# A delta-rule attention block followed by a SiLU MLP: in the first chunk, two of the four batches are joined first and alone, and two pieces of w_in meet their 128 tokens between the joins of the other two

## The chip, the cores and the metric

The kernel runs on one core of a Trainium2 chip. The metric is device time in microseconds; the time before is the median of three runs.

The engines are TensorE (PE; its weight loads are the rows PEld), VectorE (DVE), ScalarE (ACT), GpSimd (POOL) and SyncE (SP), which issues most of the DMAs. Each engine runs its own list of instructions in order, and they meet at semaphores.

## What is computed

```python
# q, k, v: (4, 8, 768, 48) float32; beta: (4, 8, 768)
k_n = k / (norm(k, axis=-1) + 1e-06)
state = zeros(4, 8, 48, 48); y = zeros_like(q)
for t in range(768):
    y[:, :, t] = einsum('bhd,bhde->bhe', q[:, :, t], state)
    v_old = einsum('bhde,bhd->bhe', state, k_n[:, :, t])
    state += beta[:, :, t] * einsum('bhd,bhe->bhde', k_n[:, :, t], v[:, :, t] - v_old)
x = y.transpose(0, 2, 1, 3).reshape(3072, 384)
h = x @ w_in                    # 384 x 2048
g = h * (1 / (1 + exp(-h)))
out = g @ w_out                 # 2048 x 384
```

## The kernel before

**Tiling.** The 768 steps are cut into six chunks of 128 (c), each chunk into two halves of 64 steps (hf). Batches 0 and 1 make group g = 0, batches 2 and 3 group g = 1; a group has 16 heads, and one half of it holds 2 x 64 = 128 tokens. One half of a chunk gives the MLP 256 tokens: 128 of each group. Within a chunk the recurrence becomes a triangular system per head, so the kernel needs the inverse of a triangular matrix for each head.

**Chunk 0, from the inverse to the first outputs.** `invert_first` (L663) inverts the small diagonal blocks on VectorE and turns them with two transposes (L690, L694). Then come the joins, which put the blocks together into the inverse of each half. Each stage is a row of small matmuls on TensorE, 16 or 32 for a group, then copies out of PSUM on ScalarE (L544) and VectorE (L547), one side of the 128 partitions each:

- `corner` (matmuls L717, copies by VectorE L724);
- `turned` (L733) and `straight` (L746), copies into xe_y and into xi;
- `merge_half`, twice (L806): the first merge reads turned's xe_y and writes xe_y, the second reads xe_y and xi and writes xi.

`joins(hf, between)` runs these stages for both groups in turn, corner(0), corner(1), turned(0), turned(1) and so on, and between them does what the list `between` holds (narrowing steps, sizing v on GpSimd by `size_half`). Then `masks` (L1364) cuts the scores of queries with a triangle (four VectorE instructions), `solve(0)` does `inner` (L840, the inverse times v), and `first_outputs` (L884), which makes the 128 tokens of one group in two PSUM banks; a ScalarE copy and a VectorE add (L893) put them into xT. `inner` writes to a zeroed strip (`slab`) and to z.

**The MLP.** `hidden(c, hf)` (L1046) goes through w_in in eight pieces f of 256 columns. A piece is six matmuls of 128 x 128 weights by 256 tokens, two halves of three with a `yield` between; in fp32 each matmul is two passes in the profile, so a half piece is six rows. A silu on ScalarE (L1056) takes the bank to gT. Hidden's banks, and those of the transposes (`turn`, L500), come from two PSUM banks in rotation (M); joins use three (A) and three (CC). `project` (L1090) multiplies by w_out.

**Narrowing.** w_in and w_out arrive as 64-bit numbers and are cut to fp32 piece by piece (`narrow`): two ScalarE instructions (L233, L234), two VectorE ones (L238, L242) and one on GpSimd (L246). `begin_next` starts ScalarE's part of the next piece in the queue, and `fill(n)` does n more of its steps; hidden's piece f needs ("in", f) narrowed. Raw pieces land in the space of tiles that are used later, and a full queue of pieces waits for that space.

**Order.** Nothing is reordered by a scheduler: `pin` (L78) puts each instruction behind the one that the program wrote before it on the same engine, and `in_line` does the same for SP's DMAs. The order is that of the program, and after the joins of half 0 it is a text that `script` (L1509) reads word by word: s is a step of `solve`, jN N matmuls of `joins(1)`, r half a piece of hidden (`run`), fN narrowing steps, b `begin_next`, q the transposes of one batch of chunk 1's queries (their ScalarE copy writes stage, L510), h the sizing of v for half 1. `project` and the steps of later chunks follow in the same text.

**Loads by count.** `pin` counts TensorE's instructions (2 for a transpose, 4 for a matmul); when the count passes the first number in `loads`, that load is issued behind the TensorE instruction reached. The numbers are WINDOW + PACKET * k + an offset, with PACKET 256 and WINDOW 445. The block loads of chunk 0 (`block_in`, L582) and those of k, v and the first two pieces of w_in are issued ahead of that.

## Time and profile before

| | |
|---|---|
| median of three runs | 641.6 us (639.44 to 643.4) |
| span of the profiled execution | 636.1 us, from the first to the last instruction |
| TensorE busy (PE / PEld) | 622.4 us / 547.3 us |
| VectorE / ScalarE / GpSimd busy | 397.5 / 214.3 / 89.9 us |
| mean granted TensorE clock | 0.986 |
| DMA | 54.70 MB, mean 86 GB/s |

The profiled execution has a span of 636.1 us and no time of its own beside it in the table; the median of the runs lies 5.5 us above the span, for what is ahead of the first instruction and behind the last.

How to read the lines that follow. `L840` is a line of the kernel before. A row of the timeline has the start in us from the span's start, the duration, engine, line, operation, the tiles written and read, and in brackets how long the engine was idle just before and who released it. "x6" is a count; rows with a count are merged. The chain of waits is followed back from the last instruction and shows what set the time at each moment; "issue" in it is time in which the engine waited for nothing that the profile shows. PEclk is the clock that TensorE was granted, as a share of full speed.

### The profile page before, as it was taken

Reading aid. Unit: us, or ns where it says so; the run is one execution under the profiler, and the core shown is the slowest. Engines: PE = TensorE matmul, PEld = TensorE weight load, DVE = VectorE, ACT = ScalarE, POOL = GpSimd, SP = SyncE. Lnnn points to the kernel's source line nnn. Section 1 sums busy time; section 2 is a strip of 40 time slices with the busy share of each in tenths; the row PEclk is TensorE's granted clock in tenths of the full one; section 3 lists DMA queues with packets and bytes.
Section 4 is the critical chain, followed back from the end, with each engine's and each line's share of the span. In section 5 each row is a group of like instructions: output and inputs, shape, how many; then the busy total and the mean of one; then the engine's idle time right before and its main releaser. Section 6 shows DMA issues by size and latency. Waiting matters only on the chain.

```text
span 636.1 us, 21387 instructions
## 1 busy us (share of the span) xinstructions
PE 622.4 (98%) x9406; PEld 547.3 (86%) x9406; DVE 397.5 (62%) x910; ACT 214.3 (34%) x500; POOL 89.9 (14%) x92
## 2 busy tenths in 40 slices
PE   7979999999999999999999999999999999999997
PEld 5568788656799989989989989989989989989997
DVE  5786879999677974546974555975455964112112
ACT  3456673423351122451122451122451122441120
POOL 5033721345020020020020010020002000000000
PEclk9779999999999999999999999999999999999999
DMA  7966726350458460459151359232253133010101
GB/s 114 227 159 177 218 67 148 100 99 4 95 105 174 72 104 8 94 107 183 37 91 21 75 124 164 56 84 29 64 117 76 26 75 37 16 38 1 26 0 26
DMA packets 145676, 54.70 MB, mean 86 GB/s; under 512 B 117152, under 2 KB 138912, under 8 KB 145584
## 3 DMA queue, kind: packets, MB, share of 16 engines
q1 hardware_dynamic: 143136, 52.93, 40.5%
q8 instruction: 74, 1.21, 0.8%
q10 hardware_dynamic: 2448, 0.41, 0.4%
q14 instruction: 18, 0.15, 0.1%
HBM read 40.14 MB, written 11.01 MB: 80 GB/s over the span
## 4 chain that ended last, share of the span: by engine, by line
PE 94%; DVE 2%; DMA 1%; issue 1%; ACTq 0%; ACT 0%; POOL 0%; SPq 0%; DVEq 0%; POOLq 0%
PE phid L1046 40%; PE px L1163 17%; PE py L1163 13%; PE po L1090 5%; PE pb_c L840 3%; PE pa L529 2%; PE pb_c L828 2%; PE pyc L919 2%; PE pb_c L1090 2%; PE pb_c L860 2%; PE pyc L906 1%; PE px L782 1%; PE py L782 1%; PE pt L500 1%; DMA sums_of_w<-blocks 1%
## 5 line engine op out<-in xcount | busy, mean ns | idle before, releaser
L1046 PE MATMUL phid<-xT,w_in 128*128 128x256 f32 x1152 | 257.0, 381 | 0.2 <-DVE xT L893 0.2
L1046 PEld LDWEIGHTS phid<-xT,w_in 128*128 128x128 f32 x1152 | 216.4, 190 | 30.2 <-issue 0.9
L1056 ACT ACTIVATE gT<-phid 128x512 f32<-128x512 f32 x88 | 52.5, 597 | 144.8 <-PE phid L1046 140.5
L1144 DVE TENSOR_TENSOR sums_of_g<-gT 128x384 f32<-128x384 f32 (+1 forms) x60 | 30.4, 529 | 65.7 <-ACT gT L1056 55.4
L627 DVE SCALAR_TENSOR_TENSOR rank<-g,step,x 128x31 f32<-128x31 f32 (+15 forms) x124 | 49.8, 401 | 21.7 <-DMA g<-blocks 18.1
L1163 PE MATMUL px<-sums_of_w,sums_of_g 128*128 128x192 f32 x320 | 56.6, 329 | 0.0
L1163 PE MATMUL py<-w_out,sums_of_g 128*128 128x192 f32 x320 | 56.2, 328 | 0.0
L1163 PEld LDWEIGHTS py<-w_out,sums_of_g 128*128 128x128 f32 x320 | 52.3, 190 | 0.3
L1163 PEld LDWEIGHTS px<-sums_of_w,sums_of_g 128*128 128x128 f32 x320 | 52.2, 190 | 0.4
L632 DVE TENSOR_TENSOR x<-x,rank 128x31 f32<-128x31 f32 (+15 forms) x124 | 42.5, 342 | 4.3
L467 POOL TENSOR_TENSOR vf<-vf,n_slot 128x768 f32<-128x768 f32 x10 | 14.8, 1494 | 174.4 <-DMA vf<-in_v_dram 150.4
L544 ACT COPY xT<-pyc 48x128 f32<-48x128 f32 (+2 forms) x126 | 32.7, 260 | 1.7
L488 DVE STREAM_TRANSPOSE kq<-stage 128x512 f32<-128x512 f32 x28 | 28.4, 1115 | 5.2 <-DMA stage<-in_q_dram 5.2
L1163 PE MATMUL py<-w_out,gT 128*128 128x192 f32 x160 | 28.9, 330 | 0.0
L1174 DVE TENSOR_TENSOR o<-o,kept 128x192 f32<-128x192 f32 (+1 forms) x29 | 11.5, 422 | 26.7 <-ACT kept L1171 26.7
L1163 PE MATMUL px<-w_out,gT 128*128 128x192 f32 x160 | 27.9, 327 | 0.0
L1163 PE MATMUL px<-sums_of_w,gT 128*128 128x192 f32 x160 | 27.8, 327 | 0.0
L1163 PEld LDWEIGHTS px<-w_out,gT 128*128 128x128 f32 x160 | 26.5, 190 | 0.6
L550 POOL COPY g<-x 64x256 f32<-64x256 f32 x4 | 5.0, 1242 | 151.9 <-DVE x L635 151.9
L1163 PEld LDWEIGHTS py<-w_out,gT 128*128 128x128 f32 x160 | 26.1, 190 | 0.4
L865 DVE TENSOR_TENSOR state<-state,pb_c 128x384 f32<-128x384 f32 x22 | 11.2, 550 | 24.1 <-PE pb_c L860 24.1
L1163 PEld LDWEIGHTS px<-sums_of_w,gT 128*128 128x128 f32 x160 | 26.2, 190 | 0.1
(222 smaller groups left out, 931.2 us busy)
## 6 DMA issues: line engine op xcount, KB each, us to landing
vf<-in_v_dram SPq DMA_DIRECT2D x48, 96.0 KB, 2.8
out_dram<-o SPq DMA_DIRECT2D x42, 96.0 KB, 2.2
w_out<-in_moe_w_in_dram SPq DMA_DIRECT2D x4, 768.0 KB, 4.7
sums_of_w<-in_moe_w_out_dram SPq DMA_DIRECT2D x4, 768.0 KB, 4.1
blocks<-ap SPq DMA_DIRECT2D x44, 64.0 KB, 1.9
g<-blocks SPq DMA_DIRECT2D x5, 512.0 KB, 3.5
kb<-in_k_dram SPq DMA_DIRECT2D x12, 192.0 KB, 4.2
kb<-in_k_dram SPq DMA_DIRECT2D x24, 96.0 KB, 4.3
```

The lines of the kernel that those rows point to most:

```text
L467: pin(nc.gpsimd.tensor_tensor(out=vf, in0=vf, in1=of, op=ALU.mult))
L488: pin(nc.vector.transpose(out=kqs[c, b][:, :, j, :].rearrange("p a (i m) -> p a m i", i=T), in_=src.rearrange("p a (m d) -> p a m d", d=D) ...
L529: pin(nc.tensor.matmul(pa[e][half, p * n * W : (p + 1) * n * W], lhsT=kq[rows, p, 0, half], rhs=kq[rows, p, js[0] : js[-1] + 1, half], sta ...
L544: return pin(nc.scalar.copy(to, of))
L627: pin(nc.vector.scalar_tensor_tensor(out=tv, in0=g[:, 0:m, m : m + 1].to_broadcast([P, m, n]), scalar=step[:, m : m + 1], in1=x[:, m : m + ...
L632: yield pin(nc.vector.tensor_tensor(out=x[:, 0:m, m:T], in0=x[:, 0:m, m:T], in1=tv, op=ALU.add))
L840: yield pin(nc.tensor.matmul(pz[rows, n * D : (n + 1) * D], lhsT=xis[g][rows, u * H + 2 * p + e, :], rhs=vfs[c][rows, hf, g * HB + u, p, : ...
L1046: pin(nc.tensor.matmul(ph[:, j * GT : (j + 1) * GT], lhsT=w_in[:, a, (2 * f + j) * P : (2 * f + j + 1) * P], rhs=xTs[c, hf][:, a, :], star ...
L1056: pin(nc.scalar.activation(out=hidden_of(c, hf, f), in_=ph[:], func=ACTF.Silu, scale=-0.5 if in_blocks(c) else 0.5))
L1090: pin(nc.tensor.matmul(pos[i][:, 0:DM], lhsT=hidden_of(0, hf, f // 2)[:, at : at + C], rhs=w_outs[f // HFF][:, f % HFF, :], start=(f == 0) ...
L1144: pin(nc.vector.tensor_tensor(out=sums_of_g[:, k, fs], in0=of[0], in1=of[1], op=op))
L1163: pin(nc.tensor.matmul(to, lhsT=at, rhs=quarter(f, *b) if isinstance(b, tuple) else sums_of_w[b][:, f], start=start and f == 0, stop=f == ...
```

## The change

- **Order of chunk 0.** `joins` no longer holds half 0 (nor the corners of half 1). Group 0 goes alone through corner, turned, straight, first merge, second merge, `inner` and `first_outputs`; then group 1 through the same stages. Between group 1's stages stand other things: the corners of half 1 (`corner(0, 1)`, `corner(1, 1)`) and two calls of `early`.
- **`early(f, g)`** multiplies piece f of w_in (f = 0, 1) with the 128 tokens of one group alone: six matmuls by 128 tokens instead of six by 256. `early(0, 0)` stands between corner and turned of group 1, `early(1, 0)` between its first and second merge; `early(0, 1)` and `early(1, 1)` come after its `first_outputs`, each with the silu. `hidden(0, 0)` then begins at f = 2. Each piece has one PSUM bank of M, held from the first call to the second.
- **Masks.** Group 0's two masks go to VectorE right after v's load is issued, ahead of the blocks' inverse; group 1's two go to GpSimd, after group 0's outputs.
- **Sizing of v** (half 0) goes ahead of the memset of `slab` on GpSimd; before it was behind.
- **Loads.** w_in 2 to 5 at packets 2 to 5, then chunk 1's queries at 6 and 7, w_in 6 at 8, w_in 7 at 10, w_out 2 at 11. Before: w_in 2 and 3 at packets 2 and 3, the queries at 4 and 5, w_in 4 to 7 at 6 to 9, w_out 2 at 10.
- **Script.** The head of the text is new: all four query transposes (q) come after the joins of half 1 have begun, where two of them stood ahead; one `r` fewer stands near the beginning of the rest, since four half pieces were done by `early`.

```diff
     def solve(c):
         if c == 0:
-            together(inner(0, 0, 0, CC))
-            together(inner(0, 1, 0, M))
-            yield
-            first_outputs(0)
-            yield
-            first_outputs(1)
-            yield
             together(update(0, 0, 0), update(0, 1, 0))
...
+    def early(f, g):
+        if g == 0:
+            early_banks[f] = bank(M, "phid")
+        ph = early_banks[f]
+        for j in range(2):
+            for a in range(NKT):
+                pin(nc.tensor.matmul(
+                    ph[:, j * GT + g * C : j * GT + (g + 1) * C],
+                    lhsT=w_in[:, a, (2 * f + j) * P : (2 * f + j + 1) * P],
+                    rhs=xTs[0, 0][:, a, g * C : (g + 1) * C], start=(a == 0), stop=(a == NKT - 1),
+                ))
+        if g == 1:
+            silu(0, 0, f, ph)
...
     def hidden(c, hf):
-        for f in range(NFF // 2):
+        for f in range(EARLY if (c, hf) == (0, 0) else 0, NFF // 2):
...
     def masks(g, u):
         to = aps[0, g][1][:, u]
-        pin(nc.vector.tensor_tensor(
+        pin((nc.gpsimd if g == 1 else nc.vector).tensor_tensor(
             out=to, in0=to, in1=above[:].unsqueeze(1).to_broadcast([P, H, W]), op=ALU.mult
         ))
...
     load_v(0)
+    masks(0, 0)
+    masks(0, 1)
...
         (WINDOW + PACKET * 2 + 15, fetch_w_in, 2),
-        (WINDOW + PACKET * 3 + 90, fetch_w_in, 3),
-        (WINDOW + PACKET * 4 + 15, load_q, 1, slice(HB * 0, HB * 0 + HB)),
-        (WINDOW + PACKET * 5 + 0, load_q, 1, slice(HB * 1, HB * 1 + HB)),
-        (WINDOW + PACKET * 6 + -15, fetch_w_in, 4),
-        (WINDOW + PACKET * 7 + -15, fetch_w_in, 5),
+        (WINDOW + PACKET * 3 + 15, fetch_w_in, 3),
+        (WINDOW + PACKET * 4 + 15, fetch_w_in, 4),
+        (WINDOW + PACKET * 5 + 15, fetch_w_in, 5),
+        (WINDOW + PACKET * 6 + 15, load_q, 1, slice(HB * 0, HB * 0 + HB)),
+        (WINDOW + PACKET * 7 + -15, load_q, 1, slice(HB * 1, HB * 1 + HB)),
         (WINDOW + PACKET * 8 + -15, fetch_w_in, 6),
-        (WINDOW + PACKET * 9 + -45, fetch_w_in, 7),
-        (WINDOW + PACKET * 10 + -15, fetch_w_out, 2),
+        (WINDOW + PACKET * 10 + -15, fetch_w_in, 7),
+        (WINDOW + PACKET * 11 + -15, fetch_w_out, 2),
...
     corner, turned, straight = next(inv)
+    size_half(0, pins[seen_on])
+    begin_next()
     pin(nc.gpsimd.memset(slab, 0.0))
...
-    together(joins(0, [...]))
-    masks(0, 0)
-    masks(0, 1)
+    together(corner(0, 0))
+    together(turned(0, 0))
+    together(straight(0, 0))
+    together(merge_half(0, 0, False))
+    fill(2)
+    together(merge_half(0, 0, True))
+    together(inner(0, 0, 0))
+    fill(1)
+    first_outputs(0)
     masks(1, 0)
     masks(1, 1)
+    fill(2)
+    together(corner(1, 0))
+    early(0, 0)
+    fill(1)
+    begin_next()
+    together(turned(1, 0))
+    together(straight(1, 0))
+    together(merge_half(1, 0, False))
+    together(corner(0, 1))
+    early(1, 0)
+    together(merge_half(1, 0, True))
+    fill(2)
+    together(corner(1, 1))
+    together(inner(0, 1, 0))
+    fill(1)
+    first_outputs(1)
+    begin_next()
+    for f in range(EARLY):
+        early(f, 1)
...
-        "s f3 s q q s j32 b j20 r f j8 q f j4 f j16 r j44 b j4 q j4 r f r j22 f j12 f j8 f b j8 f j4 r j20 e r f j99 h f r f2 l s l r l p r l f p l s l2 f r3 l3 p ...",
+        "j16 j16 r f2 b j32 r f j16 f q j48 f r q f b j16 f j16 e r f q q j99 h f f2 l s l r l p r l f p l s l2 f r2 l3 p ...",
```

The rest of the text, which is not shown, is the same in both.

More of the change, by code (lines that the diff above doesn't have):

```diff
@@ L1037, in hidden_of, with silu @@
         return gTs[f // FG][:, f % FG, :]
+    def silu(c, hf, f, ph):
+        if f % FG == 0 and (c, hf) != (0, 1):
+            gTs[f // FG] = mlp.tile([P, FG, 2 * GT], FP32, name="gT", bufs=3)
+        pin(nc.scalar.activation(
+            out=hidden_of(c, hf, f), in_=ph[:], func=ACTF.Silu, scale=-0.5 if in_blocks(c) else 0.5
+        ))
+    EARLY, early_banks = 2, {}
+    def early(f, g):
+        assert ("in", f) in narrowed
+        if g == 0:
[7 more added lines that the diff above has]
+                    rhs=xTs[0, 0][:, a, g * C : (g + 1) * C], start=(a == 0), stop=(a == NKT - 1),
+                ))
+        if g == 1:
+            silu(0, 0, f, ph)
     def hidden(c, hf):
-        for f in range(NFF // 2):
+        for f in range(EARLY if (c, hf) == (0, 0) else 0, NFF // 2):
             assert ("in", f) in narrowed
@@ L1053, in hidden @@
                     yield
-            if f % FG == 0 and (c, hf) != (0, 1):
-                gTs[f // FG] = mlp.tile([P, FG, 2 * GT], FP32, name="gT", bufs=3)
-            pin(nc.scalar.activation(
-                out=hidden_of(c, hf, f), in_=ph[:], func=ACTF.Silu, scale=-0.5 if in_blocks(c) else 0.5
-            ))
+            silu(c, hf, f, ph)
             if (c, hf, f) == (1, 0, 2 * FG) or (c > 0 and (hf, f) == (1, 2)):
@@ L1296, in first_score @@
             block_out(0, b // HB)
+    PACKET, WINDOW = 256, 445
     busy(3)
@@ L1312, with masks @@
     beta_of(0)
+    def masks(g, u):
+        to = aps[0, g][1][:, u]
+        pin((nc.gpsimd if g == 1 else nc.vector).tensor_tensor(
+            out=to, in0=to, in1=above[:].unsqueeze(1).to_broadcast([P, H, W]), op=ALU.mult
+        ))
     def first_queries(b):
@@ L1343 @@
         first_queries(b)
-    PACKET, WINDOW = 256, 445
     loads.extend((
         (WINDOW + PACKET * 2 + 15, fetch_w_in, 2),
-        (WINDOW + PACKET * 3 + 90, fetch_w_in, 3),
-        (WINDOW + PACKET * 4 + 15, load_q, 1, slice(HB * 0, HB * 0 + HB)),
-        (WINDOW + PACKET * 5 + 0, load_q, 1, slice(HB * 1, HB * 1 + HB)),
-        (WINDOW + PACKET * 6 + -15, fetch_w_in, 4),
-        (WINDOW + PACKET * 7 + -15, fetch_w_in, 5),
+        (WINDOW + PACKET * 3 + 15, fetch_w_in, 3),
[3 more added lines that the diff above has]
+        (WINDOW + PACKET * 7 + -15, load_q, 1, slice(HB * 1, HB * 1 + HB)),
         (WINDOW + PACKET * 8 + -15, fetch_w_in, 6),
-        (WINDOW + PACKET * 9 + -45, fetch_w_in, 7),
-        (WINDOW + PACKET * 10 + -15, fetch_w_out, 2),
+        (WINDOW + PACKET * 10 + -15, fetch_w_in, 7),
+        (WINDOW + PACKET * 11 + -15, fetch_w_out, 2),
         (WINDOW + PACKET * 15 + 45, fetch_w_out, 3),
@@ L1360 @@
     inv = invert_first(step)
-    def masks(g, u):
-        to = aps[0, g][1][:, u]
-        pin(nc.vector.tensor_tensor(
-            out=to, in0=to, in1=above[:].unsqueeze(1).to_broadcast([P, H, W]), op=ALU.mult
-        ))
     for n in range(1 + Q):
@@ L1381, with joins @@
     corner, turned, straight = next(inv)
+    size_half(0, pins[seen_on])
+    begin_next()
     pin(nc.gpsimd.memset(slab, 0.0))
-    def joins(hf, between=()):
+    def joins(hf):
         for stage in (
-            corner(0, hf), corner(1, hf), turned(0, hf), turned(1, hf), straight(0, hf), merge_half(0, hf, False),
+            turned(0, hf), turned(1, hf), straight(0, hf), merge_half(0, hf, False),
             straight(1, hf), merge_half(1, hf, False), merge_half(0, hf, True), merge_half(1, hf, True),
@@ L1390, in joins @@
             yield from stage
-            for what in between[:1]:
-                what()
-            between = between[1:]
-    def filled(n):
-        return lambda: fill(n)
-    def sized():
-        size_half(0, pins[seen_on])
-        begin_next()
-    def none():
-        pass
-    together(joins(0, [
-        lambda: (size_half(0, pins[seen_on]), begin_next(),),
-        lambda: (),
-        lambda: (),
-        lambda: (fill(1), fill(1),),
-        lambda: (fill(1),),
-        lambda: (),
-        lambda: (fill(1),),
-        lambda: (fill(1), begin_next(),),
-        lambda: (),
-        lambda: (),
-    ]))
-    masks(0, 0)
-    masks(0, 1)
+    together(corner(0, 0))
[7 more added lines that the diff above has]
+    first_outputs(0)
     masks(1, 0)
     masks(1, 1)
+    fill(2)
[17 more added lines that the diff above has]
+        early(f, 1)
     pieces = chained(hidden(0, 0), hidden(0, 1), project())
     needed = chained(
-        (("in", i // 2 % NWI) for i in range(4 * NWI)), (("out", i // 4) for i in range(4 * NWI))
+        (("in", i // 2 % NWI) for i in range(2 * EARLY, 4 * NWI)), (("out", i // 4) for i in range(4 * NWI))
     )
@@ L1572 @@
     for text in (
-        "s f3 s q q s j32 b j20 r f j8 q f j4 f j16 r j44 b j4 q j4 r f r j22 f j12 f j8 f b j8 f j4 r j20 e r f j99 h f r f2 l s l r l p r l f p l s l2 f r3 l3 p l s l4 p l2 s r l f l4 f l f l2 p l s l2 s p f r f r l r l2 g i p l p f i p f l i r2 i r v f i3 r3 i r i r i3 b r2 f2 r2 i r2 i2 r2 i f b i r i3 f2 r2 f r3 f i2 r f i f r3 f r f i f i2 r i r i k i2 b z r2 i r i r z r i r2 b r t s r b r f s r2 t s m r m t2 r b m f t m s f b r m2 b m f s r m r s m4 s m3 c m4 s r t G m r2 m4 V m s r m r m t2",
+        "j16 j16 r f2 b j32 r f j16 f q j48 f r q f b j16 f j16 e r f q q j99 h f f2 l s l r l p r l f p l s l2 f r2 l3 p l s l4 p l2 s r l f l4 f l f l2 p l s l2 s p f r f r l r l2 g i p l p f i p f l i r2 i r v f i3 r3 i r i r i3 b r2 f2 r2 i r2 i2 r2 i f b i r i3 f2 r2 f r3 f i2 r f i f r3 f r f i f i2 r i r i k i2 b z r2 i r i r z r i r2 b r t s r b r f s r2 t s m r m t2 r b m f t m s f b r m2 b m f s r m r s m4 s m3 c m4 s r t G m r2 m4 V m s r m r m t2",
     ):
```

## The prediction

> **What bounds the kernel now.** I read the page first.

> ```profile
> span 636.1 us, 21387 instructions
> ...
> PE 622.4 (98%) x9406; PEld 547.3 (86%) x9406; DVE 397.5 (62%) x910; ACT 214.3 (34%) x500; POOL 89.9 (14%) x92
> ...
> PE 94%; DVE 2%; DMA 1%; issue 1%; ACTq 0%; ACT 0%; POOL 0%; SPq 0%; DVEq 0%; POOLq 0%
> ```

> TensorE is the bound: 94% of the chain that ended last. Its instruction order from the second half's joins on is nearly the same in both kernels, so the end moves by what TensorE loses, or saves, before that point. The page's share (98%) hides where it is lost; the windows view shows it (columns: stretch, length, PE, PEld, DVE, ACT and POOL busy with counts, granted clock, DMA share, GB/s).

> ```profile
> 36.00:38.00 2.00, 1.90 (x129) 1.76 (x129) 1.58 (x5) 0.72 (x2) 2.00 (x2) 1.00 0.29 49
> 38.00:40.00 2.00, 0.95 (x59) 0.86 (x52) 1.92 (x4) 0.73 (x2) 0.37 (x1) 0.61 0.87 303
> 42.00:44.00 2.00, 1.03 (x39) 1.03 (x40) 1.27 (x3) 1.95 (x4) 0.78 (x1) 0.50 0.91 326
> 48.00:50.00 2.00, 2.00 (x63) 1.93 (x62) 1.87 (x4) 0.87 (x3) 0.00 (x0) 0.83 0.09 20
> 50.00:52.00 2.00, 2.00 (x142) 1.76 (x142) 1.26 (x3) 1.76 (x4) 1.91 (x1) 1.00 0.89 174
> 56.94:58.16 1.22, 1.22 (x98) 1.18 (x97) 0.42 (x1) 1.11 (x4) 0.00 (x0) 1.00 0.90 292
> ```

> In the joins TensorE is half idle, and its granted clock is 0.50 from about 38.4 (0.61 in 38 to 40) to 48.7 (0.83 in 48 to 50). The last row prices small matmuls at full clock: 16 of turned and 32 of straight, two passes each, in 1.22 us. The chain of waits gives the pieces and the end of the stretch.

> ```profile
> 38.09 1.05 issue
> ...
> 41.62 1.35 issue
> ...
> 44.83 1.88 PE pb_c L840 x32
> ...
> 52.46 1.53 PE phid L1046 x6
> ...
> 55.52 1.49 PE phid L1046 x6
> ...
> 73.95 0.70 PE pb_c L529 x32
> ```

> The first w_in matmul starts at 52.46, and from there the chain is TensorE. Two gaps of 1.05 and 1.35 us in the joins have no releaser. So the question is when TensorE becomes dense, with how much of the w_in work behind it, and whether the new order opens gaps later.

> **The change, part by part.** *One group alone.* In the old order each stage of batches 2 and 3 covers the copies of batches 0 and 1. In the new one, each stage waits for the copies of the stage before. Rows for the copies (timelines of ACT, DVE and POOL) and for the matmuls:

> ```profile
> 36.70 0.36 ACT L544 COPY xe_y<-pl 32x256 f32<-32x256 f32 x1 [1.46 <-PE pb_c L733]
> ...
> 46.80 0.48 ACT L544 COPY sums_of_w<-pb_c 128x384 f32<-128x384 f32 x1 [1.52 <-PE pb_c L840]
> ...
> 51.25 0.48 ACT L544 COPY xT<-py 128x384 f32<-128x384 f32 x1 [0.23 <-PE py L884]
> ...
> 59.76 0.56 ACT L510 ACTIVATE stage<-pt 128x512 f32<-128x512 f32 x1
> ...
> 63.03 0.92 ACT L233 ACTIVATE w_in<-w_out 128x768 f32<-128x768 f32 x1
> 63.86 0.99 ACT L234 ACTIVATE w_out<-w_out,plus 128x768 int32<-128x768 uint32 x1
> ...
> 71.70 0.60 ACT L1056 ACTIVATE gT<-phid 128x512 f32<-128x512 f32 x1
> ...
> 74.62 0.65 ACT L544 COPY ap<-pb_c 128x256 f32<-128x256 f32 x2 [1.48 <-PE pb_c L529]
> ```

> ```profile
> 22.06 0.69 DVE L668 TENSOR_TENSOR sums_of_w<-sums_of_w,step 128x512 f32<-128x512 f32 x1 [3.01 <-DMA sums_of_w<-blocks]
> ...
> 35.61 0.36 DVE L724 SCALAR_TENSOR_TENSOR sums_of_w<-pb_c,second,pick 64x128 f32<-64x128 f32 x1
> ...
> 38.95 0.87 DVE L547 COPY xi<-pb_c 32x256 f32<-32x256 f32 x2
> ...
> 45.32 2.50 DVE L1364 TENSOR_TENSOR ap<-ap,above 128x512 f32<-128x512 f32 x4
> ...
> 51.76 0.56 DVE L893 TENSOR_TENSOR xT<-xT,py 128x384 f32<-128x384 f32 x1 [0.74 <-ACT xT L544]
> ...
> 53.85 0.69 DVE L238 TENSOR_SCALAR w_in<-w_in 128x768 uint32<-128x768 uint32 x1
> ...
> 59.13 0.96 DVE L242 SCALAR_TENSOR_TENSOR w_in<-w_out,w_in 128x768 uint32<-128x768 uint32 x1
> ```

> ```profile
> 54.06 1.90 POOL L246 TENSOR_TENSOR w_in<-w_in,w_out 128x768 int32<-128x768 int32 x1 [2.06 <-DVE w_in L242]
> ...
> 72.54 1.60 POOL L385 TENSOR_TENSOR sq<-kb 128x384 f32<-128x384 f32 x2
> ```

> ```profile
> 49.24 1.09 PE L500 MATMUL pt<-ident,sums_of_g 128*128 128x128 f32 x8
> 50.26 0.93 PE L884 MATMUL py<-ap,sums_of_w 64*64 64x64 f32 x48
> ```

> ```profile
> 48.01:48.71 0.70, 0.70 (x24) 0.70 (x26) 0.52 0.08 23
> ```

> ```profile
> 21.40:22.20 0.80, 0.80 (x5) 0.47 (x3) 0.50 1.00 376
> ```

> The last two are windows of L884 and of L500 alone, at half clock: 0.029 us a pass for L884, and 0.16 or more for a 128-wide pass, which at full clock takes 1.09 / 8 = 0.136; I take 0.20 at half (bounds 0.16 and twice 0.136). A small matmul is 1.22 / 48 = 0.025 us at full clock, 0.05 at half. A handover costs about 0.1 us (the copy ends at 51.73, the add starts at 51.76 and ends at 52.32, the matmul starts at 52.46).

> Batches 0 and 1 alone: the first corner copies end at 35.97 (35.61 + 0.36) as before, since they stand behind the transposes. Turned and straight to 37.25; the two xi copies (0.87) to 38.25; the first merge's copy (0.43) to 38.7; second merge at half clock (0.8) to 39.6, with VectorE's narrowing (0.95 at most) beside it; its copy to 40.1; inner (1.88) to 42.1; its copy (0.48) to 42.65; the outputs, 48 x 0.029 = 1.4, to 44.1; xT (0.48 + 0.56) to 45.3. GpSimd's part of w_in piece 0 comes after VectorE's z copy and L242 (0.56 + 0.96, from 42.2) and takes 1.90: 45.7. So the first 128-token piece starts at 45.75; 12 passes x 0.20 = 2.4: 48.15. Its 12 corner copies and 32 corner matmuls lie beside xT.

> Batches 2 and 3, at full clock from 48.7: turned and straight to 49.4; xi copies to 50.4; the merge's copy to 50.85. Beside these copies TensorE does the merge, the corner of the next half (0.8) and the second 128-token piece (12 x 0.136 = 1.6), to 52.3; second merge (0.4) 52.7; corner (0.8) 53.5; inner (half of 1.88, since the clock doubles) 54.45; VectorE's copy, behind xi, a 0.69 narrowing and two corner copies, 55.2; outputs (0.93) 56.2; xT (0.48 + 0.56 and handovers) 57.4, with nothing for TensorE in those 1.2 us; the two pieces' other tokens, 24 x 0.136 = 3.25: about 60.6. The old kernel has the same work done (two pieces, 4 x 1.49 = 5.96, and 12 corner matmuls, 0.3, less the 8 transposes of L500, 1.09, that it does earlier and the new one later) at 52.46 + 5.2 = 57.65. The chain loses 2.9 us. Bounds: with no handovers (15 of 0.1) and a 128-wide pass at 0.16, 0.9; with twice the handovers, 4.4.

> In that sum the gaps of 1.05 and 1.35 are gone: they stand where small matmuls ran at their fastest, and the new order spreads them out. If both return, 2.4 more.

> *Edits costed at nothing.* Masks: four took 2.50 us of VectorE; two go into its wait of 3.01 us for the blocks, two to GpSimd, by L385 0.80 x 512 / 384 = 1.07 us each, between pieces 0 and 1; piece 1 is then ready at about 49.9 (45.7 + 2.1 + 1.9 and a wait for L242) and needed at 50.7. Without that 0.8 us of cover the second piece waits. Memset and sizing of v trade places on GpSimd, idle then. Loads: w_in 3 to 5 come earlier on SP's queue, the queries later (issued near 53 and 57.5, needed at 66), w_in 7 from 63.3 to about 77.

> ```profile
> w_out<-in_moe_w_in_dram SPq DMA_DIRECT2D x4, 768.0 KB, 4.7
> ```

> By this row w_in 7 lands near 82, just when ScalarE comes to it (below); a microsecond later costs a microsecond.

> *New waits after the chain.* ScalarE and TensorE each run in order, and the new script sets other neighbours. (1) The second merge of batches 2 and 3 in half 1 (L806) needs ScalarE's copy xe_y; ahead of that copy stand the stage copy of the transposes just before (0.56) and a narrowing (L233 and L234, 63.03 to 64.85 = 1.82). Handover 0.1, 0.56, 1.82, 0.36, less 0.4 that TensorE has to do: 2.45. In the old order a w_in half of 1.49 stood there too. (2) The third stage transposes take the PSUM bank of the w_in piece whose last matmul is right ahead: handover and the silu, 0.1 + 0.60 = 0.7. (3) The keys (L828) wait for a score copy; ahead of it now stand the silu (0.60) and the narrowing of w_in 7 (1.82): 0.1 + 0.60 + 1.82 + 0.33 + 0.1 - 0.70 of L529 still to do = 2.25. Before, the same wait was

> ```profile
> PE pb_c L828 <- ACT ap L544: 0.4, 1, 0.4
> ```

> so 1.85 more. Each is bounded below by zero (if ScalarE comes earlier than I have it) and above by its sum plus a late load of about 1. Behind each, TensorE's whole queue stands.

> Sum: 2.9 + 2.45 + 0.7 + 1.85 = 7.9 us. After 100 us TensorE is dense to the end, so nothing gives it back. The profiled execution has a span of 636.1, so 644.0 after; the median of the runs, 641.6, lies 5.5 above the span, and goes to 649.5.

> **The rivals.** (B) Only the chain loses: ScalarE is ahead and the three waits vanish. For it: ACT is busy 34%. Against: the order is fixed, and the copy ahead waits for TensorE itself. 641.6 + 2.9 = 644.5. (C) The clock falls again after the chain's thin stages (52 to 55.5 looks like 36 to 38, after which it fell): outputs + 0.5, 24 passes x 0.064 = 1.5: 2.0 more, 651.5. (D) Faster: the gaps of the joins swallow the pieces as drawn. Then the other tokens start at 52.46, where w_in starts now, and the waits are nil: 57.4 - 52.46 = 4.9 less chain, 2.9 - 4.9 = -2.0, 639.6. It decides from a start at 54.5 (57.4 - 2.9) on. Against: it needs batches 2 and 3 to pass seven dependent stages with no more delay than both groups have now. (E) The clock stays full through the joins: inner 0.95, merge 0.4, outputs 0.45, piece 12 x 0.064 = 0.8 less, 2.6 in all: 646.9. [...] Against: it fell at 38.4 with PE busy 1.90 of 2.00 us.
> [...]

> **How the numbers follow.** My forecast 0.50, B 0.18, C 0.16, E 0.08, D 0.08. The predicted time is 649.5. The range, 643.5 to 654, leaves out D and the far ends: below, B with a chain 1 us shorter; above, C with the two issue gaps. A measurement of this kernel can tell about 1% (6.4 us; faster under 635.2, slower over 648.0) from no change. Over 648.0 lie three quarters of the forecast and most of C, 0.53; under 635.2 hardly anything, 0.02; the rest, 0.45, within.

> **What would show it.** The first 128-token matmul near 45.7 and its other tokens near 57.4; granted clock 0.50 until 48.7; TensorE waits of about 2.4 on ScalarE's xe_y, 0.7 at the third transposes and 2.2 at L828; no issue gap in the first joins. It is wrong if the other tokens start before 54.5, or if those waits are missing.

## The result, and the profile after

The changed kernel took 663.99 us (median of 4 runs, 663.51 to 664.73), the kernel before 641.88 (639.44 to 643.4): a ratio of 1.036, 95% interval 1.0332 to 1.0389. It is slower, as forecast, but by 22.1 us where 7.9 were worked out, and lies above the range (643.5 to 654). The profiled execution has a span of 661.7 us, 25.6 more than that of the kernel before. Every timed run on record lies 1.7 to 1.8 us above its span, so the profiled execution of the kernel before took about 638 us, some 4 less than its median: most of the 5.5 us between its span and the median is this, and what is counted against that profile below comes to some 3.5 us more than the medians show. The page of the changed kernel:

```profile
span 661.7 us, 21436 instructions
...
PE 630.5 (95%) x9430; PEld 554.3 (84%) x9430; DVE 395.9 (60%) x908; ACT 213.7 (32%) x500; POOL 92.9 (14%) x94
...
PE 89%; DMA 3%; DVE 3%; issue 2%; ACT 1%; POOL 1%; SPq 0%; ACTq 0%; DVEq 0%; POOLq 0%
```

TensorE is still the bound, but its idle time grew from 13.7 us (636.1 - 622.4) to 31.2 (661.7 - 630.5), and it was busy for 8.1 us more. So 17.5 us more went into waits, and 8 into more passes and passes done more slowly. Where? Both kernels end with the same matmuls, so I counted back from the last one and compared when the same matmul starts:

| same matmul, by its time in the kernel before | later after | grown since | predicted |
|---|---|---|---|
| 62.7 (behind the chain and the first two pieces) | 10.6 | 10.6 | 2.9 |
| 85.4 (behind the three waits) | 19.3 | 8.7 | 5.0 |
| 106.1 | 20.7 | 1.4 | 0 |
| the end | 25.6 | 4.9 | 0 |

At the first mark the new order has already done 12 whole w_in passes more than the old one and 12 passes of L500 less, which by the rows of the prediction is 12 x 1.49 / 6 less 12 x 1.09 / 8, so 1.3 us of work that is not lost: 9.3 of the 10.6 belong to the chain, and 10.0 instead of 8.7 to the stretch of the waits. At 85.4 and behind it both have done the same work, but for the split of the two pieces.

The chain of waits of the changed kernel, start and length, with the longest pieces of the first stretch:

```profile
45.87 2.93 PE phid L1050 x12
51.59 1.53 PE phid L1050 x12
53.88 2.01 issue
56.40 1.66 PE pb_c L840 x32
58.77 1.65 PE py L884 x46
61.52 5.49 PE phid L1050 x24
```

L1050 are the 128-token passes; L1065 below are the passes of the whole pieces, and L1036 is their silu. The first ones start where they were expected, the second ones 0.9 us later (51.59 instead of 50.7); then comes a gap without a releaser, in the corner stage, and the other tokens start at 61.52 instead of 57.4 and take 5.49 us instead of 3.25. The waits of TensorE from 60 to 125 us (in total, times, longest):

```profile
PE px L806 <- ACT xe_y L544: 2.1, 1, 2.1
PE pb_c L828 <- ACT ap L544: 1.9, 1, 1.9
PE phid L1065 <- DMA xT<-part: 1.3, 1, 1.3
...
PE pb_c L840 <- issue: 0.8, 1, 0.8
PE pt L500 <- ACT gT L1036: 0.7, 1, 0.7
```

The three waits that were worked out (2.45, 0.7 and 2.25) are there with 2.1, 0.7 and 1.9. Their price is not. The windows view of the changed kernel, cut at multiples of 3.41 us (columns as in the prediction; the granted clock is the third number from the end):

```profile
53.29:56.70 3.41, 1.40 (x106) 1.29 (x99) 1.36 (x3) 0.36 (x1) 0.00 (x0) 1.00 0.71 234
56.70:60.12 3.42, 2.70 (x76) 2.54 (x71) 1.97 (x4) 0.48 (x1) 0.28 (x1) 0.50 0.52 98
63.53:66.94 3.41, 3.41 (x19) 3.19 (x17) 0.00 (x0) 0.60 (x1) 0.00 (x0) 0.50 0.63 114
66.94:70.35 3.41, 3.41 (x136) 2.89 (x136) 2.50 (x5) 2.91 (x5) 0.00 (x0) 1.00 0.01 1
77.18:80.59 3.41, 1.64 (x37) 1.50 (x38) 2.19 (x4) 2.05 (x4) 1.55 (x2) 1.00 0.32 51
80.59:84.01 3.42, 2.67 (x11) 1.79 (x9) 0.51 (x1) 1.17 (x2) 3.42 (x2) 0.50 0.46 184
90.83:94.25 3.42, 1.53 (x66) 1.37 (x65) 1.44 (x5) 3.42 (x6) 2.41 (x3) 1.00 0.66 216
94.25:97.66 3.41, 3.41 (x10) 2.71 (x9) 3.03 (x14) 0.48 (x1) 0.00 (x0) 0.50 0.55 98
```

Each window in which a gap of about 2 us left TensorE busy for 1.40 to 1.64 of 3.41 us is followed by half clock, and full clock returns behind a window that is busy throughout (3.41 us in that from 63.53 to 66.94). The clock was at half from 36.2 to 49.9, 56.7 to 66.9, 80.6 to 87.4 and 94.3 to 97.7: 34.1 us, where the kernel before has 10.2 in that part of its span (38.4 to 48.7). So such a wait seems to be paid twice: once as itself and once as the half-clock stretch behind it.

The growth at the end has rows too. From 126 us on the waits view of the kernel before has no row for TensorE; that of the changed one has:

```profile
PE pb_c L828 <- issue: 1.7, 1, 1.7
PE pb_c L840 <- issue: 1.1, 1, 1.1
PE px L1178 <- issue: 0.5, 2, 0.3
PE pb_c L860 <- issue: 0.4, 1, 0.4
```

Nothing in the program releases them. The page's DMA part names something else that feeds TensorE, its instructions (packets, MB, share):

```profile
q8 instruction: 74, 1.21, 0.8%
```

Each of these packets has 16 KB (1.21 MB / 74). With 9430 matmul passes and as many weight loads, 18,860 instructions over 74 packets are 255 each, and they keep step with 256: when packet k starts, counted from 0, between 152 and 430 more than 256 k of them have begun (154 to 400 in the kernel before). At every gap behind 126 us TensorE resumed 2.3 to 2.9 us after such a packet's transfer had begun (in the corner stage too: packet at 53.60, resumed at 55.89). How many packets TensorE holds at a time no run here shows. My theory for the end, call it P: the split pieces add 12 matmuls, two passes each, so 48 instructions, and from there on each packet ends at another place of the work. Where a packet holds only small matmuls, it would be used up before the next one has come. The rival for the end is that it follows from the clock, the loads or the new order. For the stretch before 100 us theory C is that the clock follows TensorE's busy share in the window before, so that the waits bring the half-clock stretches; its rivals are that the tiny tiles do it, busy or not, or that the dependent copies alone make the chain late.

### The profile page after: what moved, and what is told of

The parts are those of the page before. It is cut to its first block, busy times and chain, and to the rows that moved or that the text cites. A ratio compares the mean times of both kernels' runs of the same rounds, so it can differ in the third digit from the quotient of the medians.

```text
span 661.7 us, 21436 instructions
## 1 busy us (share of the span) xinstructions
PE 630.5 (95%) x9430; PEld 554.3 (84%) x9430; DVE 395.9 (60%) x908; ACT 213.7 (32%) x500; POOL 92.9 (14%) x94
## 3 DMA queue, kind: packets, MB, share of 16 engines
q8 instruction: 74, 1.21, 0.8%
## 4 chain that ended last, share of the span: by engine, by line
PE 89%; DMA 3%; DVE 3%; issue 2%; ACT 1%; POOL 1%; SPq 0%; ACTq 0%; DVEq 0%; POOLq 0%
PE phid L1065 36%; PE px L1178 16%; PE py L1178 12%; PE po L1105 5%; PE pb_c L840 3%; PE pa L529 2%; PE pb_c L828 2%; PE pyc L919 2%; PE pb_c L1105 2%; PE phid L1050 2%; PE pb_c L860 1%; PE pyc L906 1%; DMA kb<-in_k_dram 1%; PE px L782 1%; PE py L782 1%
## 5 line engine op out<-in xcount | busy, mean ns | idle before, releaser
L1065 PE MATMUL phid<-xT,w_in 128*128 128x256 f32 x1128 | 254.6, 384 | 1.3 <-DMA xT<-part 1.3
L1065 PEld LDWEIGHTS phid<-xT,w_in 128*128 128x128 f32 x1128 | 213.8, 192 | 31.7 <-DMA xT<-part 1.7
L1036 ACT ACTIVATE gT<-phid 128x512 f32<-128x512 f32 x88 | 52.3, 597 | 150.6 <-PE phid L1065 142.4
L1178 PE MATMUL py<-w_out,sums_of_g 128*128 128x192 f32 x320 | 56.2, 328 | 0.0
L1178 PEld LDWEIGHTS py<-w_out,sums_of_g 128*128 128x128 f32 x320 | 52.3, 190 | 0.3
L544 ACT COPY xT<-pyc 48x128 f32<-48x128 f32 (+2 forms) x126 | 32.6, 259 | 1.7
L840 PEld LDWEIGHTS pb_c<-vf,xi 64*64 64x64 f32 x768 | 25.4, 141 | 5.9 <-issue 5.1
L840 PE MATMUL pb_c<-vf,xi 64*64 64x48 f32 x768 | 27.3, 225 | 2.5 <-issue 2.4
## 6 DMA issues: line engine op xcount, KB each, us to landing
w_out<-in_moe_w_in_dram SPq DMA_DIRECT2D x4, 768.0 KB, 4.5
sums_of_w<-in_moe_w_out_dram SPq DMA_DIRECT2D x4, 768.0 KB, 4.4
```

What stands on the lines that cost most here:

```text
L544: return pin(nc.scalar.copy(to, of))
L840: yield pin(nc.tensor.matmul(pz[rows, n * D : (n + 1) * D], lhsT=xis[g][rows, u * H + 2 * p + e, :], rhs=vfs[c][rows, hf, g * HB + u, p, : ...
L1036: pin(nc.scalar.activation(out=hidden_of(c, hf, f), in_=ph[:], func=ACTF.Silu, scale=-0.5 if in_blocks(c) else 0.5))
L1065: pin(nc.tensor.matmul(ph[:, j * GT : (j + 1) * GT], lhsT=w_in[:, a, (2 * f + j) * P : (2 * f + j + 1) * P], rhs=xTs[c, hf][:, a, :], star ...
L1178: pin(nc.tensor.matmul(to, lhsT=at, rhs=quarter(f, *b) if isinstance(b, tuple) else sums_of_w[b][:, f], start=start and f == 0, stop=f == ...
```

## The experiments

All are single-core and against the kernel before on the same chip. "Tiny" matmuls are 32 x 32 x 16; the added ones write columns that nobody reads.

```
+    def pads(n, size=T, wide=Q, tag=None, after=None):
+        for _ in range(n):
+            op = nc.tensor.matmul(
+                kept_banks[tag or CC[0]][0:size, 512 - wide : 512], lhsT=ident[0:size, 0:size],
+                rhs=states[0][0:size].rearrange("p u a w -> p (u a w)")[:, 0:wide], start=True, stop=True,
+            )
...
```

**Packet ends alone: 12 tiny matmuls in the kernel before** (at its first w_in matmul), and 64 of them in its inverse.

```
-        "s f3 s q q s j32 b j20 r f j8
+        "s f3 s q q s j32 b j20 P12 r f j8
```

> The kernel before, with 12 tiny extra matmuls (32 x 32 x 16, two passes each, results unused) right ahead of the first w_in matmul, where TensorE waits 1.2 us for xT. They give TensorE's instruction stream the same 48 extra instructions (24 passes and 24 weight loads) that the split pieces give it, and nothing else. Theory P (the late gaps without a releaser in the changed kernel, 4.8 us in all after 126 us, come from where TensorE's instruction packets of 256 end): the same gaps appear here at the same places of the work (L840 and L906 of chunk 2, L828 of chunk 3 among them), +3 to +5 us, about 646. Rival (those gaps follow from clock, loads or the new order of the first joins): no such gap, 0 to +0.5 us, about 642.

Measured: 649.39 against 640.7, ratio 1.011 (1.0087 to 1.0134): 8.7 more, not 3 to 5. Of the three places named, the gaps came at L840 and L828; L906 had none. Counted against the profile before, 5.2 us were lost by 106.1 (its clock came back 3 us later, at 51.7) and 6.9 behind it. From 126 us on:

```profile
PE pb_c L828 <- issue: 1.8, 2, 1.7
PE pb_c L840 <- issue: 0.9, 1, 0.9
PE pyc L919 <- issue: 0.7, 1, 0.7
```

The longest one also brought the clock down, in the middle of the kernel:

```profile
440.79:444.20 3.41, 1.75 (x32) 1.63 (x25) 2.46 (x5) 0.50 (x1) 0.00 (x0) 1.00 0.05 8
444.20:447.61 3.41, 3.41 (x12) 3.41 (x12) 0.00 (x0) 0.27 (x1) 0.00 (x0) 0.50 0.00 0
```

The control:

```
+        if n in (5, 6, 7, 9):
+            pads(16, tag="c0", after=done)
```

> The kernel before with 64 of the same tiny matmuls (results unused) in TensorE's idle time during the inverse: 256 instructions, one whole packet, so that every later packet ends where it does in the kernel before. It is the control of the run with 12 of them, which lost 8.7 us. Theory P (the place of the packets' ends counts): no late gap, 0 to +1 us, about 641.5. Rival (extra instructions cost by their number, as more to fetch): at least as much as the 12 did, 649 or more.

Measured: 642.96 against 639.44, ratio 1.0055 (1.0037 to 1.0074): more than the 0 to 1 us expected. But of the 3.4 us by which its span is longer, 3.2 were lost by 51.5 us, where its clock stood at half for other windows (29.6 to 36.5 and 39.9 to 53.5): the tiny matmuls kept TensorE busy for all of the window from 26.2 to 29.6, yet the clock fell behind it, and the first corner matmul came at 36.2 instead of 33.6. Its page counts 75 instruction packets instead of 74. Behind 106 us nothing is lost, although there are five times as many extra matmuls as in the run before it. P holds for this stretch, and their number is not the cost there.

**The changed kernel with whole packets.** First 52 tiny matmuls in the inverse (the same lines with 13), which with the 12 of the split pieces make 256 instructions:

> The changed kernel with 52 tiny matmuls (32 x 32 x 16) in TensorE's idle time during the inverse at 22 to 33 us. With the 12 matmuls that the split pieces add they make 64, so 256 instructions, one whole packet: from the pieces' end on the packets end where they do in the kernel before. Theory P: the gaps at 179.9, 364.7, 368.2, 455.2 and 571.1 vanish, 4 to 5 us less after 126 us, about 659. The gap of 2.0 at 53.9 in the corner stage moves by 12 matmuls and may stay. Rival (the late gaps have another cause): they stay, 664.

Measured: 664.23, ratio 1.0356 (1.0337 to 1.0375), no faster. Yet the late waits are gone: from 126 us on no row is left. Behind 106 us it lost 0.4 instead of 4.9. What was won there was lost ahead of it: the clock fell behind the window that the tiny matmuls fill, although they kept TensorE busy.

```profile
28.24:31.65 3.41, 3.41 (x82) 2.84 (x81) 3.00 (x13) 0.00 (x0) 0.36 (x1) 1.00 1.06 267
31.65:35.07 3.42, 3.42 (x32) 2.31 (x32) 3.38 (x3) 0.00 (x0) 0.28 (x1) 0.50 0.97 136
```

The first corner matmul came at 38.9 instead of 33.0, and from 31.7 to 72.6 the clock was at half for 30.7 us. Then with the extra matmuls where they should also move the corner stage's packet end:

```
+    pads(12)
     first_outputs(0)
...
+    pads(18)
     early(0, 0)
...
+    pads(22)
     for f in range(EARLY):
```

> The changed kernel with 30 tiny matmuls in the waits ahead of the outputs of batches 0 and 1 and of the first 128-token piece, and 22 in the wait for xT of batches 2 and 3 (results unused). The 30 bring the packet's end that fell in the corner stage at 53.9 to the second 128-token piece, the 52 together with the split pieces' 12 make one whole packet for all that follows. Theory P with C: the gap of 2.0 at 53.9 is gone or under 0.7; TensorE's busy share in that window stays up, so the clock does not fall at 56.7 (5.1 us); the late gaps (4.8) are gone too; some 0.5 to 1 is lost to extra matmuls that outlast the waits. About 653 (651 to 657). Rival (the gap in the corner stage comes from the load traffic beside it, and the clock falls for the chain's thin stages in any case): 659 to 664.

Measured: 664.12, ratio 1.0382 (1.0359 to 1.0406). The late gaps are gone again, but for one of 0.3, while the gap of the chain came at another place (1.4 us, ahead of 58.8), and the clock stayed at half from 34.1 to 71.6, although TensorE was busy in all of the 10.2 us from 44.3 to 54.5. The expectation fell: moving packet ends cured the end and not the chain.

All profiles together, by added TensorE instructions ahead of 106 us; "lost" is how much later the last matmul is than the one at 106.1, against the kernel before:

| added instructions | kernels | lost behind 106 us |
|---|---|---|
| 0, 256 or 260 | eight kernels here | -0.1 to 1.6 |
| 16 | wide matmuls in the old joins | 3.0 |
| 48 | the changed kernel and three more | 4.5 to 6.9 |
| 88 | corner stages moved, waits filled | 11.9 |
| 100 | ballast in the waits | 7.1 |

**ScalarE's order alone.** The waits at L806 and L828 are taken away by emitting the copies ahead of the narrowings.

```
-j48 f r q f b j16 f j16 e r
+j49 f r q f b j15 f j16 e r
...
-l p r l f p l s
+l p r l p l s f
```

> The changed kernel with ScalarE's order alone changed: the copy of the first merge (half 1) goes ahead of the stage copy and the narrowing, and the last score copies go ahead of the narrowing of w_in 7. TensorE's order is the same but for one matmul. Theory C (the granted clock follows TensorE's busy share in the 3.41 us before it, so a wait of 2 us is paid a second time as a stretch at half clock): the waits of 2.1 (L806) and 1.9 (L828) shrink to under 0.7 each, and the half-clock stretches 80.6 to 87.4 and 94.3 to 97.7 vanish with them: 3 to 4 us of waits and 5.1 us of clock, together 8 to 9 less, about 655.5. Rival (the clock falls for the small tiles or the order of the work itself, whatever the waits): the stretches stay, 3 to 4 less, about 660.5.

Measured: 662.91, ratio 1.033 (1.0303 to 1.0358). Both waits are gone (0.3 is left at L828), but another came at the scores, on VectorE:

```profile
PE pb_c L529 <- DVE state L865: 1.7, 1, 1.7
```

With it the window from 82.0 had TensorE busy for 1.67 us, and the clock fell behind it as before, and twice more behind windows busy for 2.09 and 2.04 (to half at 99.0 and 112.7). So the expectation failed although nothing in it speaks against its mechanism: one 2 us wait gave way to another.

**The waits filled.** Seven and six 128 x 128 matmuls in front of the two waits.

```
-f b j16 f j16 e r
+f b j16 f H7 j16 e r
...
-l f p l s
+l f p l I6 s
```

> The changed kernel with 7 extra 128 x 128 matmuls in front of the wait at L806 (76.8) and 6 in front of the wait at L828 (90.9), results unused: some 1.8 and 1.6 us of TensorE time inside waits of 2.1 and 1.9. The waits' ends stay where they are. Theory C: with the waits filled the clock does not fall at 80.6 and 94.3, so 5.1 us less by 100 us (up to 1 of it lost if the extra matmuls outlast a wait); after that the 52 added instructions move the packets' ends again, by -4 to +3. Rival (ScalarE's lateness alone is the loss, or small tiles bring the clock down): no less at 100 us, 0 to +1.

Measured: 664.86 in the median (658.75 to 667.95), ratio 1.0351 (1.0313 to 1.039). In the profile the waits are filled, down to 0.4 and 0.3, and the clock stays:

```profile
76.56:79.97 3.41, 2.99 (x67) 2.71 (x60) 1.92 (x4) 2.76 (x5) 1.72 (x1) 1.00 0.22 19
79.97:83.38 3.41, 2.66 (x46) 2.01 (x48) 1.19 (x2) 1.32 (x3) 3.10 (x2) 1.00 0.58 217
```

By 85.4 the loss is 14.8 instead of 19.3: 4.5 of the 5.1 us that the half-clock stretches were said to cost. Behind 106.1 it lost 7.1 us, where the change lost 4.9, so with its 52 new instructions 2.2 of the gain went there. This is a run of 660.7 us, one of the two quickest of its six; the slower four, which make the median no better than the change's, have no profile.

**The order behind the chain alone.** The first joins as in the kernel before, the pieces whole, and everything behind them as changed.

```
-    together(corner(0, 0))
-    together(turned(0, 0))
...
+    together(both(corner, 0))
+    together(both(turned, 0))
...
+    together(inner(0, 0, 0, CC))
+    together(inner(0, 1, 0, M))
...
-        "j16 j16 r f2 b
+        "r4 j16 j16 r f2 b
```

> One part alone: the first joins in the order of the kernel before (both groups together, w_in pieces 0 and 1 whole behind them), but everything behind them in the order of the changed kernel, its loads and masks too. It separates what the chain of one group alone costs from what the new neighbours behind it cost. If the waits behind the chain (2.1, 0.7, 1.9) and the half-clock stretches that follow them are a loss of their own: they appear here too, 4.3 us of waits and 5 of clock, and the packets end as in the kernel before: about 650 (647 to 653), so that the chain has the other 10 to 12 us of the change. Rival (the late chain is what brings the waits about, by shifting ScalarE's work): the waits are absent and the time is 641 to 644.

Measured: 650.86 against 639.59, ratio 1.0175 (1.0158 to 1.0193), within the range expected. The waits are the same to a tenth:

```profile
PE px L806 <- ACT xe_y L544: 2.1, 1, 2.1
PE pb_c L828 <- ACT ap L544: 1.9, 1, 1.9
PE phid L1065 <- DMA xT<-part: 1.7, 1, 1.7
...
PE pt L500 <- ACT gT L1036: 0.7, 1, 0.7
```

Its clock was at half from 74.2 to 81.0 and from 87.9 to 91.3, behind the two long waits, as in the changed kernel. So half of the change's loss needs no chain of one group at all. Not all of it lies behind the joins, though: here too the first joins were longer at half clock (36.7 to 57.2, where the kernel before has 38.4 to 48.7). Of the 15.7 us by which its span is longer, 4.3 are there at the mark of 62.7 (1.3 of them work done earlier, as in the change), 10.4 come between 62.7 and 106.1, and 1.0 behind it.

**The split pieces taken out** (order kept, pieces 0 and 1 whole behind the chain).

```
-    EARLY, early_banks = 2, {}
+    EARLY, early_banks = 0, {}
...
-        "j16 j16 r f2 b
+        "r4 j16 j16 r f2 b
```

> The changed kernel without the split pieces: the first two pieces of w_in are done whole (256 tokens) when xT of all batches is there, in the order of joins that the change made. Leaves out nothing. TensorE has 48 instructions fewer, so its packets end as in the kernel before from there on. Theory P: the late gaps (4.8) are gone; the waits of 2.1, 0.7 and 1.9 and their half-clock stretches stay. With 2.9 + 1.5 us of early passes out of the chain of batches 2 and 3 and 0.5 to 3 us more of w_in behind it, the pieces end within 2 us of 67. About 658. Rival (the split pieces are what fills the chain, as the change has it): the pieces end 3 or more later, 661 to 665.

Measured: 659.9, ratio 1.0322 (1.0297 to 1.0347). The pieces end at 69.0, two us later than the split ones, and the late gaps are gone. In the profiles the split pieces win 2 in the chain and lose 4 at the packets' ends; that the whole is some 2 us faster than the change isn't clear of noise, since the intervals of the two ratios overlap. Against the run above, the order of one group alone costs 9 us (659.9 - 650.9), and by the profiles all of it is lost by the mark of 62.7 (12.7 against 4.3).

**The masks alone** in the kernel before.

```
-    masks(0, 0)
-    masks(0, 1)
     masks(1, 0)
...
+        pin((nc.gpsimd if g == 1 else nc.vector).tensor_tensor(
```

> The kernel before with the masks alone moved: two into VectorE's wait for the blocks, two to GpSimd. The prediction costs it at nothing: 641, 0 to -1.5 (VectorE loses 2.5 us ahead of its copies of the first outputs). Rival: GpSimd's masks of 1.7 us each hold its part of w_in pieces 0 and 1 back, +1 to +3.

Measured: 640.21 against 639.44, ratio 1.0011 (0.9995 to 1.0027): nothing. The loads alone weren't tried: in the old order the queries' transposes read what they bring.

**Is it the clock in the joins?** Wide matmuls in the waits of the chain (with tiny ones up to 260 instructions), and all cures in one:

```
+    pads(1, P, DM)
     together(corner(0, 0))
...
+    pads(3, P, P)
     early(0, 0)
...
```

> The changed kernel with wide extra matmuls (results unused) in the waits of the first joins: 128 x 384 ones ahead of the first corner stage and of the corner stage that had the gap, 128 x 128 ones ahead of each merge (1), inner (1 and 0), outputs (2), the first 128-token piece (3) and the pieces' other tokens (4); and 37 tiny ones in the wait at L806, which make 256 added instructions with the rest. Theory C (the clock follows TensorE's busy share in the 3.41 us before): of 23.9 us at half clock before 67 at most 10 are left, the pieces' end comes 4 to 6 us earlier; theory P: the late gaps (4.8) are gone. About 653 (649 to 657). Rival (the thin tiles of the joins bring the clock down, busy or not): as much half clock as before, 0.5 to 2 us of extra matmuls on the path, no less than 659.

> All the cures in one: the wide matmuls in the joins as in the run beside it, ScalarE's copies ahead of the narrowings, four 128 x 128 matmuls in the wait of the third transposes, and tiny ones up to 256 added instructions. If waits, clock and packet ends are the whole loss but for the chain itself, some 4 us less than the run beside it: 649 (645 to 654), which is what the prediction gave for the change without them. Rival (an order of one group alone is starved of instructions whatever fills its waits, and new gaps appear where old ones go): 656 or more.

The wide matmuls ahead of a merge stand in the chain of batches 0 and 1 alone, and in the second kernel the tiny ones take the place of the four ahead of the pieces' other tokens.

Measured: 659.78, ratio 1.0295 (1.0258 to 1.0332), and 657.39, ratio 1.0268 (1.0247 to 1.0289). Half clock before 67 us fell from 23.9 to 13.7 in both; the last early passes start at 64.6 and 66.3 instead of 66.6. Against the kernel before that is 19 and 17 us more, where the change has 22; both expectations missed, by 7 and 8 us, and both times lie where the rivals had them. One window of the first kernel says more of what the clock follows. The wait at L806 that seven 128 x 128 matmuls had filled was filled here with 37 tiny ones. TensorE was busy for 3.34 us of the window, more than there (2.99), and the clock fell all the same, for 10.2 us:

```profile
72.96:76.37 3.41, 3.34 (x92) 2.96 (x91) 2.94 (x5) 2.31 (x4) 1.84 (x1) 1.00 0.02 5
76.37:79.79 3.42, 3.42 (x63) 3.09 (x61) 1.69 (x3) 0.70 (x2) 0.90 (x1) 0.51 0.74 210
```

So theory C does not hold as it stands: the busy time of the trace isn't what the clock follows, and the rival of the tiny tiles has its part. In the joins of the kernel before:

```
-        lambda: (),
+        lambda: (pads(1, P, DM),),
```

> The kernel before with four 128 x 384 matmuls (results unused) among its first joins, ahead of turned of batches 0 and 1, of both straight stages and of the last merges. Theory C: TensorE's busy share stays up, the stretch at half clock from 38.4 to 48.7 vanishes or shrinks to 3.4, and the gaps of 1.05 and 1.35 take up one matmul each: 1 to 4 us less, about 638. Rival (these stages are bound by the supply of instructions, not by the clock): 2.2 us of matmuls on the path, 0 to +2, 640 to 642.

Measured: 645.91 against 640.38, ratio 1.0084 (1.0062 to 1.0107). The first joins ran at full clock to 45.8:

```profile
35.60:39.02 3.42, 3.19 (x130) 2.21 (x129) 2.80 (x6) 0.72 (x2) 2.71 (x2) 1.00 0.71 151
39.02:42.43 3.41, 2.73 (x127) 2.04 (x128) 2.35 (x5) 1.45 (x4) 0.42 (x1) 1.00 0.37 141
```

and nothing was won: 2.5 us were lost by 62 us, and the 16 instructions cost 3.0 at the end. In both windows some 128 passes, as many as one packet holds, took 3.4 us at full clock. A window of the kernel before, at half clock:

```profile
38.45:41.86 3.41, 2.48 (x127) 2.35 (x128) 3.29 (x7) 1.60 (x6) 0.91 (x1) 0.50 0.64 215
```

It has as many passes, which fits stages that go at the pace of their packets, as the rival has it. It isn't proof: taken from 38.42 to 41.83, a window of the same joins with wide matmuls has 165 passes, and the time lies above what the rival gave, too.

**Is it the gap in the chain?** The corner stages of half 1 taken out of it, without and with filled waits.

```
-    together(corner(0, 1))
     early(1, 0)
...
-    together(corner(1, 1))
...
     for f in range(EARLY):
         early(f, 1)
+    together(corner(0, 1))
+    together(corner(1, 1))
```

> The changed kernel with the two corner stages of half 1 (128 tiny passes, 256 instructions) taken out of the chain of batches 2 and 3 and put behind the two pieces. Theory G (the gap of 2.0 in the corner stage and the clock that falls 0.8 us behind it are what made the chain late): no gap without a releaser between 50 and 57, no fall of the clock near 56.7, the last of the 48 early passes starts at 63 or before instead of 66.6; about 1 of that is lost again where the corner stages now stand; 658 to 660.5. Rival (the dependent copies set the chain, and TensorE with less to do between them falls to half clock all the same): last early pass at 65.5 to 68, 662 to 666.

> The same with ten 128 x 128 matmuls (results unused) in the waits ahead of the second merge, inner, outputs and other tokens of batches 2 and 3 (2, 2, 2 and 4). Theory G: as beside it or up to 1 us more, since the extra matmuls lie in waits: last early pass by 63.5, 658 to 661. Theory C alone (only the clock matters): the run beside it stays late (66 or more) and this one is early. Rival: both late.

Measured: 664.0, ratio 1.0368 (1.0333 to 1.0402), and 667.43, ratio 1.0409 (1.0385 to 1.0433). No gap is left between 50 and 57 us, but the clock was at half to 55.3 in both, and fell again at 58.8 in the first. The pieces' other tokens, first without and then with filled waits:

```profile
60.56 5.32 PE phid L1050 x24
```

```profile
60.64 2.94 PE phid L1050 x24
```

They start at 60.6 in both, one us earlier than in the change. So taking the gap away gained 1 us, the clock another 2.4 on the 24 passes, and the rest of the delay against 57.4 is in the chain of dependent stages, whose own passes run at half clock too. Theory G gave 63 and got 65.6 for the start of the last early pass, with the rival's time; with filled waits it was 63.3, as expected, but that kernel, which has 88 added instructions, lost 11.9 us behind 106.1 and with them its time (658 to 661 was expected).

## Why the prediction was wrong

The direction and the three waits were right, the size was not. The steps that failed are two: the sum took the clock as full from 48.7 us on, in the chain and behind the waits (3.7 and 5.1 us), and it put the gaps at the ends of instruction packets at nothing (2.0 us in the chain, 4.9 behind 106 us). By its steps:

- *First 128-token piece at 45.75*: 45.87, held back by GpSimd's part as worked out. Its 12 passes took 2.93, so 0.244 each, not 0.20: within the bounds given (0.16 to 0.272), the wrong choice inside them.
- *"Batches 2 and 3, at full clock from 48.7"*: the clock came back at 49.9 and fell again at 56.7. This step failed most. Inner took 1.66 (0.95), the outputs 1.65 (0.93), the other tokens 5.49 (3.25). Rival C had the mechanism at 2.0 us, without inner; by these three it was 3.7. It also priced the clock in the chain alone, not behind the waits.
- *"In that sum the gaps of 1.05 and 1.35 are gone"*: they came back as gaps of 1.3 (L733) and 2.0 (L717). I read them as a matter of speed, "where small matmuls ran at their fastest"; they look to be a matter of packets (TensorE resumed 3.1 and 2.3 us after a packet's transfer had begun), which spreading the stages out does not take away.
- *Chain 2.9 us*: 10.6 at the matmul of 62.7. The other tokens ended at 67.0 instead of 60.6, which explains 6.4 of the 7.7 too much: 3.7 in the three stages above, 2.0 in the gap, 0.5 in the first piece, and 0.2 more in handovers. The last 1.3 are the work that the new order has done earlier at that mark.
- *Waits 2.45, 0.7, 1.85*: 2.1, 0.7 and 1.5 (1.9 less the old 0.4). What failed is the step from a wait to its price: 10.0 us were lost over them instead of 5.0 (8.7 between the marks and the 1.3), since each long one brought half clock, 6.8 and 3.4 us long, which is 5.1 us of lost speed. Filling the waits gave 4.5 of it back.
- *Loads and masks at nothing*: the masks on GpSimd took 1.46 and 1.99 instead of 1.07 each, and cost nothing in the run that had them alone; w_in 7 made nobody wait. A new wait of 1.3 for xT's parts, not foreseen, is there in the kernel with only the new order behind the chain too (1.7), and, with 1.4, in the kernel before with wide matmuls in its joins, so it doesn't need the new order. Why it appears was not traced.
- *"After 100 us TensorE is dense to the end, so nothing gives it back"*: nothing gave it back, but 4.9 us more were lost. The sum treated 24 passes more as 24 passes. They are also 48 instructions, and those alone, in the kernel before, cost 1.1%, 6.9 us of it behind 106 us in the profile.
- *Rival E*: that the clock would stay full was wrong, as the rows had it. From 33 us on the stretches at half clock are multiples of 3.41 us long (10.2 before; 13.7, 10.2, 6.8 and 3.4 in the changed kernel), and where they begin differs from kernel to kernel (38.4 before, 36.2 changed). In the profiles of these two, cut into windows as above from 33 us on and without the last window, the full-clock windows in which TensorE was busy for 1.40, 1.52, 1.64, 1.84 and 2.39 us were followed by half clock (the last one in the kernel before, 35.0 to 38.4), those with 2.27, 2.37, 2.41, 2.57, 2.65 and 2.74 by full clock, as were all that were busier. The windows of 1.84 and 2.39 had no pass with 128 x 128 weights, the six that kept the clock had such passes for 0.52 us or more. With tiny matmuls added it fell behind 3.34 and 3.41 us too (72.96 and 28.24 in the rows above). Full clock came back in the two kernels only behind windows busy for all of the 3.41 us, but not behind every such window in the runs: the three from 44.3 to 54.5 in the second kernel with whole packets were followed by half clock again. So the busy time alone does not decide; the windows that go against it are made mostly of small tiles, and where the line lies stays open.

By medians the loss divides into about 11 us for the order behind the chain, with the masks, the loads and what it does to the first joins (650.9 - 639.6), 9 for the chain of one group alone (659.9 - 650.9), and 2 for the split pieces with their packet ends (1.036 against 1.0322, not clear of noise; 2 won in the chain, 4 lost at the end). Of the 11, the waits and the half clock behind them are read off the rows, and filling the waits bore out the clock's share; why the clock stayed low in the joins is not shown. The packet ends behind 106 us are shown. Of the 9, the gap and the clock are shown as parts; how much of the rest is dependence and how much the supply of instructions stays open. No kernel here beat the one before, and all cures in one gave back 5 of the 22 us.

## What to carry to other kernels

The waits of 2.1 and 1.9 us on the bounding engine here were not paid once: half clock for 6.8 and 3.4 us stood behind them. Look at the granted clock in the rows behind a wait, and where it falls, price that stretch at half clock as well. Filling such a wait helped with 128 x 128 matmuls (4.5 us by 85.4) and not with tiny ones (10.2 us at half clock). Where stages are made of tiny matmuls, count instructions as well as time: 98 passes took 1.22 us at full clock, so 128 of them, one packet, some 1.6 (an estimate), while no two packets began less than 3.28 us apart in the kernel before and 3.44 in the changed one. The 48 instructions of 12 tiny matmuls cost 6.9 us behind 106 us, 256 of them nothing there. Compare variants with added instructions brought to a multiple of 256, or else a change's merit and its luck with the packets can't be told apart.
